# Softcap attention followed by a leaky two-matmul layer, on one core: the instruction order planned anew, with another landing model for transfers and a later load of the slopes

## The chip, the cores and the metric

One core of one Trainium2 chip runs the whole program. The metric is device time in microseconds, and less is better. The engines named below are PE (TensorE, matmuls and transposes), DVE (VectorE), ACT (ScalarE), POOL (GpSimd) and SP (SyncE, which issues the loads).

## The reference

Attention over 4 batches of 12 heads, 448 tokens and 64 wide, whose output, laid out as 1792 tokens of 768, goes through a matmul, a leaky activation with one slope for each of 2048 hidden columns, and a second matmul:

```
scores = scale * np.matmul(q, k.transpose(0, 1, 3, 2))
scores = cap * np.tanh(scores / cap)
scores = scores - np.max(scores, axis=-1, keepdims=True)
attn = np.exp(scores)
attn = attn / (np.sum(attn, axis=-1, keepdims=True) + 1e-09)
x = np.matmul(attn, v)  ->  (1792, 768)
h = x @ w_in                                            # (1792, 2048)
g = np.maximum(h, 0.0) + alpha * np.minimum(h, 0.0)     # alpha: the slopes
out = (g @ w_out).astype(np.float32)                    # (1792, 768)
```

q, k and v come in 32-bit floats, w_in and w_out in 64-bit ones, so a block of 128 rows or columns of a weight is a load of 768 KB.

## The kernel before

**Numbers.** A value that goes into a large matmul is split into a high and a low half of 16 bits (hi = the rounded value, lo = value minus hi), and products are added up in three passes. A split is written in one of two forms. The two-step form is a scaled cast (`scaled`, on ACT L430, POOL L432 or DVE L434) and then one DVE instruction that scales again and subtracts (`split_lo`, L440). The three-step form scales in 32 bits (the same three lines), casts (`copy`, ACT L424 or DVE and POOL L426) and subtracts (`minus`, DVE or POOL, L437). The constants `QA` and `PA` say which share of the splits of q and k (batches 2 and 3) and of the blocks of P, the normalised attention (`turn_split`), takes the two-step form. A 64-bit weight is first turned into 32 bits by three DVE instructions on its words (L1059, L1063, L1069, in tiles `wi` and `wp`).

**Stages.** First q, k and v of batch 0 are loaded, with w_in between them. The attention of batch 0 runs in 32 bits: q and k turned (L542, PE), scores (L577, PE), tanh (L614, ACT), row maxima (L618, DVE), exp (L625, ACT), P turned (L729, PE, and copied out of PSUM into `ptall` by L424 or L426), P times V (L792 or L775, PE). Beside it w_in is turned to 32 bits, normed (L1094, PE, or L1083, ACT; maxima by L393, DVE) and split (L440). Then the first matmul of batch 0 (called mm1, L958, on tiles `wi` and `xring`) runs in pieces beside the attention of batch 1, whose q and k come through `rqk` and L896. Its leaky activation ends in DVE L968 (tile `gr`). While it runs, w_out is loaded, turned to 32 bits, normed and split. The second matmul (mm2, L999, on `wp` and `gall`) of batch 0 follows, and so on to mm2 of batch 3.

**Maxima over all partitions** (`allmax`) are a chain of four steps: a PE transpose (L410), a DVE reduction (L406, for several columns also L408), a PE matmul that spreads the result (L413), and one DVE step that takes it. `g_scales` runs such a chain for the slopes: DMA L1160 into `alph`, maximum L393 (into `small`), the chain, and five small DVE steps to L1175, which make the two columns that the leaky activation reads.

**What sets the order.** All work is given to a planner (class `Plan`) as operations with a priority and a duration for each engine that may run it. To each priority comes an entry of the table `OFF`, picked by the operation's tag. At build time the planner runs the list forward: whenever an engine is free it takes the ready operation of lowest priority, and where two engines may run it, one of them by penalties (`PEN`, `PEN2`, `PENP`). On PE it may prefer an operation of the kind that ran last, if its priority is within `SAME` of the best. For a load it keeps a time `dma` to which the queue is filled, and takes the load to have landed a fixed 1000 ns after its turn. When PE finds nothing ready, a PSUM bank is free and the planned time is under `FILL_END`, it issues a dummy matmul (`fill`, L1234). The order that comes out is fixed: on the chip each engine executes its own list in that order and waits by semaphores where a list runs ahead of another. No line of the program changes at run time.

Of the kernel before, what the change touches and what calls it, by code (L numbers as in the profile page):

```python
# [28 lines left out]
PEN = 24324.02  # L29
PEN2 = 429.82  # L30
PENP = 13233.71
B0_P = 250.67
LD_P = -207.13
LO_P = 1890.42
MM_P = 6687.03
X_P = 667.61
ST_P = 117.78
ST1_P = -42.95
PV_P = 180.1
QK_P = -338.71  # L40
V_P = 252.08
WI_P = -374.93
WI_S = -48.3
A_S = 13.82
MM1_P = 493.59
WO_P = -142.86
WO_S = 62.91
WT_P = -1745.7
WT_S = 152.86
B1_P = 620.29  # L50
B_S = 132.46
EVAC_P = -1002.09
# [14 lines left out]
QA = 1.0  # L67
# [5 lines left out]
SAME = 531.89  # L73
LOAD_C = (600, 1400, 800)
# [5 lines left out]
PA = 0.25  # L80
# [4 lines left out]
OFF = [3.2, -401.1, 51.6, -139.2, 1454.6, 45.4, 49.8, -38.2, -674.3, -24.9, 39.6, 25.1, 158.3, -197.5, -914.5, -88.5, 509.5, -178.6, 60.3, 0.0, -1155.4, -66.4, -213.9, -817.7, 80.9, 223.2, -262.7, 162.2, -263.5, -63.5, -48.8, 49.8, -256.2, 272.2, -674.8, -1321.6, 1531.5, 161.9, 273.3, 23.0, 228.0, 224.1, 138.3, 162.3, -70.6, 30.6, -8.0, -59.3, 30.1, -251.0, -100.4, 5.5, -69.7, 0.0, 190.4, 1595.1, -152.2, 194.8, -431.9, -189.3, -1491.2, -862.4, 160.4, -1336.1, 33.2, -298.2, 425.3, -180.6, 0.0, 254.3, -23.0, -3.7, 263.9, -37.4, -38.9, -2097.2, -19.9, -1.4, -1522.5, -29.8, 647.0, -1770.0, 0.0, 0.0, -2980.8, 103.4, 1914.1, -557.4, 537.1, 33.2, 0.0, -723.6, -373.5, 666.0, 575.6, -2208.6, 45.7, 308.9, -17.0, 277.2, -3.3, -236.9, -75.7, -356.6, -424.1, -182.7, -3431.1, 182.9, 247.3, 272.4, 199.8, 432.4, 188.3, 97.9, 326.3, -20.1, 35.8, 424.1, -507.3, -84.4, -664.4, -36.3, -30.7, 155.2, -3774.1, -4705.4, -2233.8, -2244.6, -3489.6, -1814.7, -1501.8, -3152.5, -2525.4, -6577.6, -3901.4, -7294.4, -6281.6, -5181.6, -5400.1, -5863.8, -9408.1, -4749.4, 31.4, -11.9, 122.6, -3734.2, -450.2, 1153.7, -124.3, -50.9, -94.9, 6155.4, 2068.9, -169.5, -343.4, -8404.7, -9228.1, -8931.4, -5436.4, -4226.4, -3789.6, -4921.0, -5305.1, -3359.5, -409.5, -2852.4, 56.1, -4291.1, -4249.4, -2856.7, -4858.0, -4928.0, -3627.5, -1585.6, -3201.7, -1945.6, -301.3, -781.1, 155.4, -5983.9, -3358.0, -3814.4, -282.7, 13.0, 89.7, 103.9, -3.1, 445.1, -30.9, -43.1, -148.3, -92.7, -159.7, -48.8, 183.8, -1697.3, -20.0, -2624.2, -1773.8, -5.0, -2469.5, 7.9, -2409.3, -2334.6, -16.3, -17.6, -2663.0, -2434.4, -2901.0, -2971.5, -2452.3, -655.0]  # L85
# [9 lines left out]
class Plan:  # L95
# [44 lines left out]
    def order(self):  # L140
        now, dma, seq = START, 0.0, 0
# [54 lines left out]
        while todo:  # L196
# [10 lines left out]
            for e in free:  # L207
# [3 lines left out]
                while ready[e]:  # L211
# [23 lines left out]
                    if e == "sp":  # L235
                        issue, wait, t = t
                        dma = max(now + wait, dma) + t
                        end = dma + 1000.0
                        lanes = lanes[1:] + [end]
                        free[e] = max(now + issue, lanes[0])  # L240
                    elif e == "pe":
                        free[e] = run_pe(t + (SWITCH + o.first if o.mode != mode else 0.0), o.rows)
                        mode = o.mode
                        end = free[e] + DRAIN
# [35 lines left out]
def kernel(  # L280
# [11 lines left out]
    nc = tc.nc  # L292
# [163 lines left out]
    def load(prio, dst, src, b, pair, w):  # L456
        op(prio, {"sp": (600, 1400, 880)}, lambda e: nc.sync.dma_start(out=dst.rearrange("p (h c) -> p h c", h=2),
                                                          in_=heads(src, b, pair)), w=w)
# [581 lines left out]
    def load_w(prio, flat, fr, i, src, split):  # L1040
# [6 lines left out]
        op(prio, {"sp": (550, 1800, (2350 if split else 1950) if wide else 1700)}, lambda e: nc.sync.dma_start(  # L1047
# [110 lines left out]
    def g_scales(prio):  # L1158
        plan.tag = -1
# [48 lines left out]

    def all_ops():
        loads32()  # L1210
        g_scales(30)
        for part in range(2):
            attention_0(part)
        for j in range(0, NF, WG):
# [67 lines left out]
```

## Time and profile before

| what | value |
|---|---|
| time, median of 3 runs | 673.92 us (673.86 to 675.18) |
| the profiled execution | 677.45 us, of which 675.7 us from the first to the last instruction (its span) |
| PE busy | 648.9 us, 96% of the span; mean granted clock 0.996 |
| DVE busy | 460.8 us (68%) |
| ACT busy | 418.3 us (62%) |
| POOL busy | 269.3 us (40%) |
| loads and stores | 87.06 MB |

An engine's busy time is the union of its instructions' spans, so waiting is not in it. The granted clock is the share of full speed that TensorE was given: 1.00 is 2.4 GHz and 0.50 is 1.2 GHz. The profiled execution lies 3.5 us above the median of the timed runs.

### The profile page before, as it was taken

How to read it: one execution, taken by the hardware profiler on the slowest of the kernel's cores; microseconds unless marked ns; L12 is line 12 of the kernel's file. 1: busy time of each engine (PE TensorE's matmuls, PEld its weight loads, DVE VectorE, ACT ScalarE, POOL GpSimd, SP SyncE). 2: the span in 40 equal slices, each digit the busy share in tenths (PEclk: the TensorE clock that was granted, in tenths of full speed). 3: DMA queues.
4: the chain of work that ended last, by engine and by line, in shares of the span. 5: the costliest groups of instructions: out<-in, count | busy, mean ns of one | idle time of the engine just before them, and what ended most of it. 6: DMA issues, size and time to landing. Idle time of an engine off the chain costs nothing. (4 is left out here: it accounts for less than half of the span.)

```text
span 675.7 us, 13258 instructions
## 1 busy us (share of the span) xinstructions
PE 648.9 (96%) x5003; PEld 410.0 (61%) x5003; DVE 460.8 (68%) x886; ACT 418.3 (62%) x868; POOL 269.3 (40%) x395
## 2 busy tenths in 40 slices
PE   8979988999999998999999999999999999999997
PEld 6768767788776555544455555544445555555664
DVE  2898999899898886688988787788884004440000
ACT  3868899789989955487867478686884013331000
POOL 0233267558777723174763445466671000000000
PEclk9999999999999999999999999999999999999999
DMA  9997945434863699558589889789766100000110
GB/s 231 277 275 180 305 131 146 149 109 151 185 92 64 115 185 194 137 104 145 94 160 205 162 190 176 146 157 161 121 104 117 40 24 25 1 0 1 30 41 23
DMA packets 190048, 87.06 MB, mean 129 GB/s; under 512 B 156256, under 2 KB 186272, under 8 KB 189984
## 3 DMA queue, kind: packets, MB, share of 16 engines
q1 hardware_dynamic: 189760, 86.12, 58.9%
q8 instruction: 39, 0.64, 0.4%
q14 instruction: 25, 0.20, 0.1%
q10 hardware_dynamic: 224, 0.10, 0.1%
HBM read 45.82 MB, written 5.51 MB: 76 GB/s over the span
## 5 line engine op out<-in xcount | busy, mean ns | idle before, releaser
L958 PE MATMUL p<-xring,wi 128*128 128x448 f16 (+2 forms) x1440 | 226.9, 315 | 2.8 <-DVE gr L968 1.7
L999 PE MATMUL p<-wp,gall 128*128 128x384 f16 x1344 | 223.9, 326 | 0.6 <-DVE gr L968 0.6
L958 PEld LDWEIGHTS <-wi 128*128 128x128 f16 x1440 | 134.7, 98 | 87.6 <-issue 9.1
L999 PEld LDWEIGHTS <-gall 128*128 128x128 f16 x1344 | 129.9, 98 | 90.2 <-issue 6.0
L625 ACT ACTIVATE tall<-tall,mxs 128x448 f32<-128x448 f32 x126 | 82.9, 660 | 24.1 <-POOL mxs L620 15.0
L968 DVE SCALAR_TENSOR_TENSOR gr<-p,ca_g,gr 128x448 f32<-128x448 f32 (+2 forms) x80 | 46.8, 585 | 58.4 <-ACT gr L430 58.0
L618 DVE TENSOR_REDUCE mxs<-tall 128x2 f32<-128x896 f32 x63 | 67.9, 1080 | 8.9 <-ACT tall L614 8.5
L620 POOL TENSOR_SCALAR mxs<-mxs,small 128x2 f32<-128x2 f32 x68 | 38.7, 570 | 60.3 <-DVE mxs L618 52.7
L437 POOL TENSOR_TENSOR pw<-tall,pw 128x448 f16<-128x448 f32 x47 | 52.5, 1123 | 21.8 <-ACT pw L424 20.5
L430 ACT ACTIVATE gr<-p,cs_g 128x448 f32<-128x448 f32 (+2 forms) x63 | 35.1, 556 | 39.5 <-PE p L958 37.3
L430 ACT ACTIVATE wp<-p,small 128x384 f32<-128x384 f32 x21 | 12.1, 577 | 65.6 <-PE p L999 65.3
L437 POOL TENSOR_TENSOR gall<-gr,gall 128x192 f16<-128x192 f32 (+4 forms) x52 | 43.9, 848 | 15.8 <-ACT gall L424 11.3
L644 POOL TENSOR_SCALAR rr<-sums 128x2 f32<-128x2 f32 (+2 forms) x70 | 25.1, 360 | 57.0 <-ACT tall L625 35.0
L614 ACT ACTIVATE tall<-s,ams 128x896 f32<-128x896 f32 x42 | 41.5, 995 | 9.0 <-POOL pw L437 4.2
L775 PE MATMUL p<-ptall,vs 112*64 112x448 f16 x384 | 41.1, 354 | 3.2 <-DMA ptall<-pw 1.8
L434 DVE TENSOR_SCALAR wp<-p,joint 128x384 f32<-128x384 f32 (+1 forms) x2 | 1.0, 512 | 60.4 <-ACT wp L430 60.4
L424 ACT ACTIVATE pw<-tall 128x448 f16<-128x448 f32 x51 | 28.7, 571 | 20.9 <-DMA ptall<-pw 18.6
L424 ACT ACTIVATE gall<-gr 128x384 f16<-128x384 f32 (+4 forms) x62 | 27.4, 448 | 21.1 <-DVE gr L968 20.7
L437 DVE TENSOR_TENSOR pw<-tall,pw 128x448 f16<-128x448 f32 x37 | 24.5, 665 | 14.9 <-ACT pw L424 13.6
L775 PEld LDWEIGHTS <-vs 112*64 112x64 f16 x384 | 21.9, 109 | 20.5 <-issue 7.9
L437 DVE TENSOR_TENSOR gall<-gr,gall 128x64 f16<-128x64 f32 (+4 forms) x60 | 27.5, 464 | 6.9 <-ACT gall L424 4.4
L432 POOL TENSOR_SCALAR tall<-tall,rr 128x448 f32<-128x448 f32 x32 | 25.3, 792 | 13.5 <-DVE rr L647 12.5
(173 smaller groups left out, 983.5 us busy)
## 6 DMA issues: line engine op xcount, KB each, us to landing
wp<-in_moe_w_in_dram SPq DMA_DIRECT2D x16, 768.0 KB, 9.1
wp<-in_moe_w_out_dram SPq DMA_DIRECT2D x16, 768.0 KB, 4.5
rvs<-in_v_dram SPq DMA_DIRECT2D x38, 224.0 KB, 3.7
rqk<-in_k_dram SPq DMA_DIRECT2D x12, 224.0 KB, 3.4
rqk<-in_q_dram SPq DMA_DIRECT2D x12, 224.0 KB, 3.2
ptall<-pw SPq DMA_TRANSPOSE x128, 3.2
wp<-in_q_dram SPq DMA_DIRECT2D x6, 224.0 KB, 8.6
wp<-in_k_dram SPq DMA_DIRECT2D x6, 224.0 KB, 8.7
```

The lines of the kernel that those rows point to most:

```text
L424: nc.scalar.activation(out=o, in_=i, func=AF.Copy)
L430: nc.scalar.activation(out=o, in_=i, func=AF.Copy, scale=s)
L432: nc.gpsimd.tensor_scalar(out=o, in0=i, scalar1=s, scalar2=1.0, op0=ALU.mult, op1=ALU.mult)
L437: (nc.gpsimd if e == "pool" else nc.vector).tensor_tensor(out=o, in0=a, in1=b, op=ALU.subtract)
L614: op(pr, {"act": (152 if reg else 245) + 377 * 2}, lambda e: nc.scalar.activation(out=t, in_=s[:, :, :S].rearrange("p c (j k) -> p c j k", ...
L618: op(pr, {"dve": 136 + 469 * 2}, lambda e: nc.vector.tensor_reduce(out=mt, in_=t, axis=AX.XY, op=ALU.max), r=tr, w=[mr], port=False)
L620: op(pr, {"dve": 200, "pool": 265}, lambda e: (nc.gpsimd if e == "pool" else nc.vector).tensor_scalar(out=mt, in0=mt, scalar1=ncap, scalar ...
L625: nc.scalar.activation(out=t[:, x], in_=t[:, x], func=AF.Exp, scale=capr, bias=mt[:, x:x + 1], accum_out=sums[:, u.idx % 3, col + x:col + ...
L775: nc.tensor.matmul(pv[x * D:(x + 1) * D, :n], vs[:, z, c:c + D], u.pt[x][:CP, y * NCH + kc], start=(i == 0), stop=(i == len(prods) - 1))
L958: nc.tensor.matmul(ps_p[h.slot][:, :n], w[:, z, kk, :], x[:, d, o:o + n], start=(kk == 0 and z == d), stop=(kk == NPAIR - 1 and z == 1))
L968: op(pr, {"dve": 198 + 1.07 * n}, lambda e: nc.vector.scalar_tensor_tensor(out=t, in0=ps_p[h.slot][:, :n], scalar=ca_g[:, j:j + 1], in1=t, ...
L999: nc.tensor.matmul(ps_p[h.slot][:, :NH], g[j][:, d, t * P:(t + 1) * P], w[:, z, hf * NH:(hf + 1) * NH], start=(j == 0 and z == d), stop=(j ...
```

## The change

Nothing is computed otherwise, apart from the form of some splits. What changes are numbers that set the order, and two rules:

- The planner's landing model. `deep` is how far the queue of loads is filled ahead of this load; a load now lands 1200 ns, plus half of `deep` up to 1600 ns, after its turn. A load of 224 KB counts 940 ns in the queue (880 before), one of w_in 2550 (2350), of w_out 2050 (1950), of the slopes 3200 (900), and the 112 KB loads of q and k in batches 1 to 3 (`LOAD_C`) 850 (800).
- `g_scales` has priority 2300 instead of 30 and a tag of its own.
- `QA` goes from 1.0 to 0: all 24 splits of q and k in batches 2 and 3 take the three-step form. `PA` goes from 0.25 to 0.75: of the 112 blocks of P, 84 take the two-step form, 28 before.
- `SAME` goes from 531.89 to 1872.02, and 22 base priorities and penalties and the whole table `OFF` (now 213 entries) have other values.

```diff
-PEN = 24324.02
-PEN2 = 429.82
-PENP = 13233.71
+PEN = 17613.56
+PEN2 = 1129.33
+PENP = 11360.55
...
-QA = 1.0
+QA = 0
...
-SAME = 531.89
-LOAD_C = (600, 1400, 800)
+SAME = 1872.02
+LOAD_C = (600, 1400, 850)
...
-PA = 0.25
+PA = 0.75
...
+                        deep = max(0.0, dma - now - wait)
                         dma = max(now + wait, dma) + t
-                        end = dma + 1000.0
+                        end = dma + 1200.0 + min(1600.0, 0.5 * deep)
...
     def load(prio, dst, src, b, pair, w):
-        op(prio, {"sp": (600, 1400, 880)}, lambda e: nc.sync.dma_start(out=dst.rearrange("p (h c) -> p h c", h=2),
+        op(prio, {"sp": (600, 1400, 940)}, lambda e: nc.sync.dma_start(out=dst.rearrange("p (h c) -> p h c", h=2),
...
-        op(prio, {"sp": (550, 1800, (2350 if split else 1950) if wide else 1700)}, lambda e: nc.sync.dma_start(
+        op(prio, {"sp": (550, 1800, (2550 if split else 2050) if wide else 1700)}, lambda e: nc.sync.dma_start(
...
     def g_scales(prio):
-        plan.tag = -1
-        op(prio, {"sp": (500, 1100, 900)}, lambda e: nc.sync.dma_start(out=alph, in_=alpha.rearrange("(j p) -> p j", p=P)), w=[("sg", 0, 1)])
+        plan.tag = 211
+        op(prio, {"sp": (500, 1100, 3200)}, lambda e: nc.sync.dma_start(out=alph, in_=alpha.rearrange("(j p) -> p j", p=P)), w=[("sg", 0, 1)])
...
-        g_scales(30)
+        g_scales(2300)
```

One line is added, so from L237 on every line of the changed kernel has a number one higher.

**On SP, the end of batch 0's loads.** Before, from the 16th row of SP's list on (`wp_93` to `wp_96` take turns at holding w_in; `wp_97` to `wp_100` hold q and k of batch 0, and later w_out):

```order
L457 DMA wp_98<-in_k_dram 112x2x256
L457 DMA vs_119<-in_v_dram 112x2x256
L1047 DMA wp_96<-in_moe_w_in_dram 128x6x256
L1047 DMA wp_93<-in_moe_w_in_dram 128x6x256
L457 DMA wp_100<-in_q_dram 112x2x256
L1047 DMA wp_95<-in_moe_w_in_dram 128x6x256
L1160 DMA alph<-in_moe_alpha_dram 128x16x1
L457 DMA wp_100<-in_q_dram 112x2x256
L1047 DMA wp_97<-in_moe_w_out_dram 128x1536
```

Afterwards, the same stretch of SP's list:

```order
L458 DMA wp_100<-in_q_dram 112x2x256 x2
L1048 DMA wp_93<-in_moe_w_in_dram 128x6x256
L458 DMA rvs<-in_v_dram 112x2x256
L458 DMA vs_119<-in_v_dram 112x2x256
L458 DMA xring<-in_v_dram 112x2x256
L1048 DMA wp_95<-in_moe_w_in_dram 128x6x256
L1161 DMA alph<-in_moe_alpha_dram 128x16x1
L1048 DMA wp_97<-in_moe_w_out_dram 128x1536
```

The last load of q has moved from behind the slopes to four loads ahead of them. At the head of the list, five loads of q and k now stand ahead of the first of w_in, three before.

**On PE, the chain of the slopes.** Before, with the scores of the last heads of batch 0 behind it (`p_63` to `p_66` are the PSUM banks, `n_wi` are the maxima of w_in):

```order
L413 MATMUL p_65<-mxt,ones 128x4
L542 MATMUL p_63<-ident,wp_100 64x112 x8
L410 MATMUL p_65<-ident,small 1x128
L413 LDWEIGHTS ones
L413 MATMUL p_65<-mxt,ones 128x1
L577 MATMUL s_61<-tall,wp_100 128x224 x4
```

Afterwards:

```order
L411 MATMUL p_63<-ident,vam 1x128
L414 LDWEIGHTS ones
L414 MATMUL p_63<-mxt,ones 128x1
L411 MATMUL p_63<-ident,small 1x128
L414 LDWEIGHTS ones
L414 MATMUL p_63<-mxt,ones 128x1
L730 MATMUL p_64<-ident,gall 112x128 x4
L730 MATMUL p_66<-ident,gall 112x128 x4
L411 MATMUL p_63<-ident,n_wi 4x128
```

The chains of v's maximum (`vam`), of the slopes and of the next norms of w_in now stand behind each other with eight transposes between them, and no dummy matmul among them. In the whole list the dummy matmuls go from 175 to 106.

**On DVE, beside the early pieces of mm1.** Before, the steps up to the leaky activation that frees the PSUM bank of the next piece of mm1, which is on wi_81 and stands behind 83.6 us of PE's own work:

```order
L387 TENSOR_SCALAR iv_wi<-p_66 128x4
L440 SCALAR_TENSOR_TENSOR wi_84<-wi_86,s_wi,wi_84 128x768
L618 TENSOR_REDUCE mxs<-ptall 128x2
L389 TENSOR_SCALAR iv_wi<-iv_wi 128x4
L440 SCALAR_TENSOR_TENSOR wi_87<-wi_89,s_wi,wi_87 128x768
L968 SCALAR_TENSOR_TENSOR gr<-p_66,ca_g,gr 128x192
```

Afterwards, the steps up to a copy of turned P in batch 1, which PE needs behind 84.3 us of its own work:

```order
L409 TENSOR_SCALAR mxt<-ident,mxt 4x4
L441 SCALAR_TENSOR_TENSOR wi_88<-wi_90,s_wi,wi_88 128x768
L388 TENSOR_SCALAR iv_wi<-p_65 128x4
L812 TENSOR_TENSOR xs<-p_66,xs 128x256
L390 TENSOR_SCALAR iv_wi<-iv_wi 128x4
L1060 TENSOR_SCALAR wp_93<-wp_94 128x768
L1140 RECIPROCAL s_wi<-iv_wi 128x4
L1064 SCALAR_TENSOR_TENSOR wp_93<-wp_94,wp_93 128x768
L619 TENSOR_REDUCE mxs<-tall 128x2
L394 TENSOR_REDUCE vam<-p_64 128x1
L648 RECIPROCAL rr<-rr 128x4
L427 COPY ptall<-p_66 112x4x128
```

The attention of batch 1 has moved ahead of pieces of mm1 (an engine's own work is the sum of its instructions in the list at the mean durations of their groups in the profile before, dummy matmuls left out): 72 matmuls of L958 stand within the first 83.6 us of PE's own work before, and within the first 100.1 us afterwards.

## Rows read from the trace of the kernel before

**Rows 1.** Page, part 1: busy us (share of the span) xinstructions.
```profile
PE 648.9 (96%) x5003; PEld 410.0 (61%) x5003; DVE 460.8 (68%) x886; ACT 418.3 (62%) x868; POOL 269.3 (40%) x395
```
**Rows 2.** The chain that ended last: start us, us, what.
```profile
504.42 7.96 PE p L999 x48
...
608.90 62.41 PE p L999 x384
```
**Rows 3.** Windows: stretch, its us, busy of each engine (count), PEclk, DMA share, GB/s.
```profile
0.00:80.00 80.00, 70.26 (x865) 59.64 (x865) 61.74 (x115) 56.35 (x120) 19.93 (x43) 0.98 0.95 248
80.00:160.00 80.00, 73.37 (x758) 61.27 (x757) 74.39 (x131) 68.63 (x159) 49.89 (x61) 1.00 0.50 151
160.00:300.00 140.00, 136.02 (x1040) 88.79 (x1038) 117.18 (x225) 107.19 (x221) 80.35 (x111) 1.00 0.68 134
300.00:520.00 220.00, 217.99 (x1456) 114.36 (x1455) 179.26 (x351) 159.05 (x324) 119.13 (x183) 1.00 0.81 149
...
660.00:675.70 15.70, 11.30 (x70) 6.58 (x68) 0.42 (x1) 1.00 (x2) 0.00 (x0) 0.94 0.11 25
```
**Rows 4.** Windows of L1234 alone, the dummy matmuls, in the first 80 us.
```profile
0.00:80.00 80.00, 13.54 (x173) 11.94 (x173) 0.98 0.95 248
```
**Rows 5.** Windows of 20 us, two of the first eight; columns as in group 3.
```profile
60.00:80.00 20.00, 19.12 (x235) 17.05 (x232) 19.91 (x34) 16.72 (x39) 6.13 (x8) 1.00 0.88 243
...
140.00:160.00 20.00, 19.16 (x210) 17.10 (x208) 19.93 (x34) 16.19 (x43) 12.79 (x16) 1.00 0.40 120
```
**Rows 6.** Waits of PE, 0 to 400 us: waited for: us, times, longest.
```profile
PE p L542 <- DMA wp<-in_q_dram: 3.0, 3, 1.3
...
PE p L958 <- DVE gr L968: 1.7, 2, 0.8
...
PE p L775 <- issue: 1.3, 1, 1.3
...
PE p L410 <- DVE vam L529: 1.0, 2, 0.8
...
PE p L775 <- DMA ptall<-pw: 0.7, 1, 0.7
```
**Rows 7.** Timeline of PE about 152 us: start, us, instruction [idle before it].
```profile
152.55 0.82 PE L958 MATMUL p<-xring,wi 128*128 128x192 f16 x8 [0.84 <-DVE gr L968]
```
**Rows 8.** Timeline of DVE, 114 to 118 us.
```profile
114.94 0.68 DVE L426 COPY ptall<-p 112x512 f32<-112x512 f32 x1
```
**Rows 9.** Waits of DVE, 0 to 207 us; columns as in group 6.
```profile
DVE wi L1059 <- DMA wp<-in_moe_w_in_dram: 8.8, 5, 4.6
...
DVE wp L1059 <- DMA wp<-in_moe_w_out_dram: 2.5, 2, 1.6
```
**Rows 10.** Timeline of DVE, 9 to 18 us.
```profile
9.58 0.56 DVE L1059 TENSOR_SCALAR wi<-wp 128x768 int32<-128x768 int32 x1 [4.57 <-DMA wp<-in_moe_w_in_dram]
```
**Rows 11.** Groups of DVE by form: line, shapes, count | busy us, mean ns.
```profile
L440 DVE SCALAR_TENSOR_TENSOR nat<-rqk,ams,nat 112x256 f16<-112x256 f32 x48 | 27.1, 614 | 0.1
L437 DVE TENSOR_TENSOR pw<-tall,pw 128x448 f16<-128x448 f32 x37 | 24.5, 665 | 14.9 <-ACT pw L424 13.6 <-POOL pw L426 0.9
L440 DVE SCALAR_TENSOR_TENSOR pw<-tall,rr,pw 128x448 f16<-128x448 f32 x28 | 19.9, 711 | 3.3 <-ACT pw L430 3.3
```
**Rows 12.** Timeline of PE, 36 to 46 us.
```profile
38.72 0.99 PE L542 MATMUL p<-ident,wp 112*64 112x112 f32 x16 [0.75 <-DMA wp<-in_q_dram]
...
40.49 1.78 PE L577 MATMUL s<-tall,wp 64*128 64x224 f32 x16
```
**Rows 13.** Windows about a pause of PE; columns as in group 3.
```profile
46.00:48.40 2.40, 0.00 (x0) 0.01 (x1) 2.40 (x3) 2.13 (x6) 1.80 (x3) 1.00 1.08 323
48.40:50.00 1.60, 1.58 (x12) 1.40 (x14) 1.60 (x4) 0.15 (x1) 0.97 (x1) 0.75 1.09 343
50.00:52.00 2.00, 2.00 (x13) 1.38 (x9) 1.34 (x2) 0.92 (x1) 0.00 (x0) 0.50 1.15 279
```
**Rows 14.** Timeline of PE, 45 to 53 us.
```profile
48.93 3.14 PE L577 MATMUL s<-tall,wp 64*128 64x224 f32 x16
```

More of the change, by code (lines that the diff above doesn't have):

```diff
@@ L28 @@
 AQ = 3
-PEN = 24324.02
-PEN2 = 429.82
-PENP = 13233.71
[L32 to L52, printed above, removed]
+PEN = 17613.56
+PEN2 = 1129.33
+PENP = 11360.55
+B0_P = 663.82
+LD_P = -321.77
+LO_P = 2106.39
+MM_P = 6096.43
+X_P = 624.32
+ST_P = 167.74
+ST1_P = -107.3
+PV_P = -101.81
+QK_P = -455.54
+V_P = 329.3
+WI_P = -299.53
+WI_S = -31.69
+A_S = 17.19
+MM1_P = 379.27
+WO_P = 157.32
+WO_S = 41.37
+WT_P = -2099.18
+WT_S = 16.53
+B1_P = 412.84
+B_S = 112.23
+EVAC_P = -1314.66
 LAT = 35.0
@@ new lines @@
+OFF = [342.6, -7.7, -9.1, 0.0, 807.2, 220.9, 0.1, -403.5, 323.1, 393.5, 0.0, 767.6, 677.3, 0.0, -463.9, 290.4, 349.0, -81.1, -18.5, -174.2, -729.8, -2084.7, -344.3, -55.5, -233.5, 178.9, 107.2, 0.0, -269.8, 0.0, -46.0, 470.5, 37.4, -33.6, -485.0, -14.4, 5306.2, 807.0, 7.2, 3536.3, 1985.2, 272.7, 4709.4, 168.0, 228.4, 1474.8, 3.7, 0.0, -5.9, -810.1, 0.0, -1.6, -559.8, -239.5, 2763.1, 176.5, 176.2, 133.4, 158.2, 136.8, 120.1, -9.3, 257.6, 650.2, 1063.2, -172.3, 52.1, -157.2, 31.7, -53.8, 29.9, 230.0, -1253.5, -685.2, -1.2, -3319.8, -1110.3, -3965.3, -5249.8, -47.2, -722.4, -459.9, -69.5, -11.9, -231.9, -1298.0, -888.9, -936.5, 2.0, 29.5, 821.0, 0.0, -487.3, 903.8, -241.8, 167.6, 154.8, 27.3, -154.0, -366.0, -424.8, -2192.9, -2021.7, -2141.0, -2584.3, -3193.3, -2956.4, -1776.7, -1206.1, -3754.8, -1921.8, -211.4, -2488.5, -2829.9, -1665.6, -2469.6, -595.1, -1496.7, -314.8, -1544.2, -3233.1, -2498.4, -1610.3, -1731.7, -1159.6, -1943.8, -1530.0, -1547.0, -1332.0, -1201.3, -130.1, -886.1, -590.1, 623.2, -72.5, -361.2, -129.3, -136.5, -932.1, -253.9, -1492.2, -50.7, -85.7, -34.0, 1158.5, 503.2, -1042.2, 651.6, 72.9, 10.7, 0.0, 2733.6, -403.7, 4746.4, -300.0, -12344.4, -12239.7, -14208.6, -10298.3, -5122.2, -4318.0, -5166.3, -6295.0, -4082.2, -258.8, -3271.3, -149.7, -5007.8, -264.1, -0.8, 298.2, -5522.1, -3915.9, 605.5, 642.8, -4.7, 361.7, 924.6, 426.0, -5199.4, -3321.6, -3754.8, -202.3, 444.7, -50.9, 0.0, 3.4, 191.8, 98.2, 73.2, -76.0, 214.6, 0.0, -182.7, -245.5, 372.0, 333.2, 2693.0, 281.9, 1329.2, 224.4, 164.1, 181.1, 2334.3, 908.9, 232.1, 756.7, -838.1, 525.8, 252.5, 544.3, 180.5, -236.4]
```

1 line of the change is left out of this document (removed).

## The prediction

> **What bounds the kernel now.** I read the busy times, then the chain of waits, then windows. PE is busy for 648.9 of 675.7 us [rows 1], and from 504.42 us on the chain is little but PE [rows 2]. So any gain or loss is in the time in which PE does not do its own work. The windows say where that lies [rows 3]: PE is idle for 9.7 us up to 80 us, 6.6 from 80 to 160, 4.0 from 160 to 300, 2.0 from 300 to 520 and 4.4 in the tail. To these come the dummy matmuls, 13.5 us, nearly all in the first 80 us [rows 4]: they fill time in which PE has nothing else, so I count them as stall. Up to 160 us PE's stall is thus 9.7 + 6.6 + 13.5 = 29.9 us, and behind that, without the tail, 6.0.
>
> Who makes PE stall? In the 20 us from 60 and again from 140 DVE is busy for 19.9 [rows 5], while PE idles, and the last such pause is PE's wait of 0.84 us at 152.55 for a DVE step [rows 7]. Up to there DVE is the bound. Most of the waits named for PE before that are short, and some of them are put down to loads [rows 6]. A load that comes late costs only what DVE does not cost anyway.
>
> This gives a sum that can be carried to another order. At a place where PE waits for DVE, PE's stall so far is DVE's work up to the step waited for, plus the time that DVE has lost, minus PE's own work ahead of the waiting matmul. The works are counts in the order by the mean durations of their groups. At 152.55 us, DVE's work ahead is 134.2 us and PE's 123.3, so DVE has lost 152.55 - 134.2 = 18.4, the lag (work against work) is 10.8, and the stall 29.2; the windows had 29.9, so such sums hold to within 0.7. Elsewhere in this stretch the lag of before is 7 to 10 us.
>
> **The change part by part.** *The sizes first.* PE's own work is the same in both orders. DVE's grows from 460.8 to 465.2 us, ACT's falls by 14.0 and POOL's by 31.0. This comes from `QA` and `PA`. Of the q and k splits, 48 DVE steps of 614 ns go, 29.5 us; of the P blocks, 56 more DVE steps of 711 ns come, 39.8, and 24 subtractions of 665 ns go, 16.0 [rows 11]; smaller shifts between engines give the rest. All of these steps stand behind 159 us of DVE's own work in either order, so they run from about 167 us on. From 160 to 520 us PE idles for 6.0 us altogether and DVE is free for 360 - 296.4 = 63.6 [rows 3]. I take the forms as worth nothing; if that cover were gone, they would cost at most their 4.4 us, and if POOL's 31 us less shorten the waits left there, they give at most the 1.5 us that remain under the covers counted below.
>
> *The slopes' load.* It moves to behind q, k and v, as all its list on SP shows. The last load of q, which stood behind it, was waited for 0.75 us [rows 12]. So the move is worth 0 to 0.75 us, and only if nothing else holds PE there. DVE bounds this stretch, so I take 0. (The Trainium skill, page "DMA: Bandwidth & Descriptors", section "Queues, rings and completion order", says that completion is not first in, first out for one issuing engine, so a small load could overtake. By that rule the slopes held nobody up and the move gives exactly 0; no row here shows an overtaking.)
>
> *The slopes' chain.* It stands on PE's list right behind that of v's maximum, with the norms next. PE's own work there is 1.7 us (38.9 to 40.6 of its total) while DVE has 7 us between the answers; there is no dummy matmul in it. This is counted in the lag, which climbs from -0.2 to 6.2 us across it. It isn't the largest lag and so costs nothing by itself.
>
> *The order on DVE and PE.* This is the term that decides. The attention of batch 1, which needs much of DVE for little of PE, has gone ahead of mm1, which needs little of DVE. At 84 us of PE's own work, DVE's work that must be done was 91.6 us (lag 8.0) and is now 99.9 (lag 15.6). At 103 and 115.6 us of PE's work the lag is 15.1 and 15.2; only behind 160 does it fall to 10.6, then 7.7 at 196. The largest lag of before was 10.8.
>
> What DVE loses is to be taken over, as no row shows it for the new order. At 99.3 us of its work it was at 115.62 us [rows 8], lost 16.3; at 134.2 us it had lost 18.4. The main loss is at the start: the first weight is waited for until 9.58 us [rows 10]. Now two loads more stand ahead of that weight. At the 248 GB/s of the first 80 us [rows 3], 2 x 224 KB (229,376 bytes each) take 1.8 us. Some 0.8 of it should be won back, since DVE next waits for the first exps in either order; so I add 0 to 1.8 and take 0.4 at the later places. The two places give 15.6 + 16.3 + 0.4 = 32.3 and 15.2 + 18.4 + 0.4 = 34.0. The larger one holds: 34.0 against 29.2, **+4.8 us** when the second matmul starts (bounds +4.4 to +6.2).
>
> *What comes back.* Of the 6.0 us of stall behind 160 us, the waits for DVE's small steps and for one transposed P, 2.7 us in all (0.83 of it the longer `vam` wait, 0.7 the `ptall` one [rows 6]), fall away when PE comes 4.8 us later against the same DVE. The wait of 1.3 that shows no releaser, and 2.0 in many small pieces, I leave as they are. So -2.7 (bounds 0 and -6.0). The tail of 4.4 us is the same mm2 and evictions.
>
> Sum: +4.8 - 2.7 = **+2.1 us**. The profiled execution would have a span of 677.8 instead of 675.7; it lies 3.5 us above the median of 673.92, so I set the sum on the median: 676.0 us. With the bounds of the two terms it lies between 4.4 - 6.0 = -1.6 and +6.2, mostly 674 to 678.7.
>
> **The rivals.** *DVE's waits go (faster).* The landing model is nearer to what the queue does. DVE's waits for w_in are 8.8 us, 4.6 of them the first, and it waits 2.5 for w_out [rows 9]. If the new order asks for each weight late enough, the 4.2 us of the later w_in waits vanish: DVE loses 14.2 instead of 18.4 at the second place and the stall there is 15.2 + 14.2 = 29.4, with 15.6 + 14.2 = 29.8 at the first one. Against 29.2 that is +0.6, and -2.7 behind it: 671.8; with all of the 6.0 gone, 668.5. For it speaks that loads of w_in get a little more room in SP's list; against it that two fifths of those waits are under 0.8 us each. The turning point is a loss of 16.7 us at 131 us of DVE's work: below it the change is faster.
>
> *All is won back (same).* If the lag of 15 us is paid but the whole 6.0 behind it goes, it is -1.2: 672.7; with half of the unreleased waits, 674.
>
> *The clock (slower).* After a pause of 2.4 us without a dummy matmul, PE was granted 0.75 and then 0.50 (1.2 GHz) [rows 13], and 16 score matmuls took 3.14 us [rows 14] against 1.78 [rows 12]. 69 dummy matmuls fewer leave such pauses open. (The Trainium skill, page "TensorE: Matmul & The Clock Gate", section "Part 1: The HAM clock gate", has the throttled clock as the default state, which activity releases; that speaks against taking fillers out, and the rows just named agree.) Where PE waits for DVE anyway a slow stretch costs nothing; where scores go through ACT to DVE it delays DVE. Two such stretches at 1.4 us each on top of the forecast: 678.8.
>
> *The change does not do what it says.* The slopes' load could be no hindrance: then only the order counts, which is my forecast without change.
>
> **How the numbers follow.** What a measurement of this kernel can tell from no change is about 0.2%, 1.35 us: same is 672.57 to 675.27. Forecast 0.47 (676.0, of which a fourth falls into same), waits go 0.25 (671.8, nearly all faster), all won back 0.15 (674, same), clock 0.13 (678.8, slower). Faster: 0.25 and 0.01 from the won-back case, 0.26. Same: 0.12 + 0.13 = 0.25. Slower: 0.35 + 0.13 + 0.01 = 0.49. The range leaves a tenth on either side: below 670.8 lies the part of the faster rival in which most of the 6.0 goes too, above 680.0 the clock rival with the upper bound of the lag.
>
> **What would show it.** Right: PE idle or on dummy matmuls for about 34 us up to the first L999, which has 177.3 us of PE's own work ahead of it and so would start near 211 us (by the same sum 177.3 + 29.2 = 206.5 before); its waits in the region of 110 to 150 us end with DVE steps; DVE over 19 busy in most windows of 20 us from 60 to 140; next to no PE idle behind 160. Wrong, to the fast side: DVE's waits for w_in summing to under 6 us, and a first L999 at or before 207.5 us. Wrong, to the slow side: granted clocks under 0.9 in more than one window of 20 us. It would also be wrong if the mean durations did not hold in the new order, for instance if DVE's steps beside POOL's took longer or shorter.

## The result, and the profile after

The changed kernel takes 666.33 us (median of 4 runs, 665.50 to 667.37) against 673.89 of the kernel before; the ratio is 0.9889, with a 95% interval of 0.9865 to 0.9913. It is faster by 7.6 us, where 2.1 us slower was forecast, and lies below the range that was given.

The profiled execution has a span of 665.6 us (675.7 before). Page, part 1, of the changed kernel (answers to [rows 1]):

```profile
PE 642.9 (97%) x4934; PEld 406.2 (61%) x4934; DVE 469.8 (71%) x885; ACT 407.0 (61%) x839; POOL 245.8 (37%) x369
```

The same windows as [rows 3], the last one moved with the end of the span (stretch, its us, busy of PE, PEld, DVE, ACT and POOL, then PEclk, DMA share, GB/s):

```profile
0.00:80.00 80.00, 69.06 (x816) 57.33 (x817) 65.94 (x124) 58.05 (x123) 26.49 (x46) 0.96 0.94 254
80.00:160.00 80.00, 75.70 (x794) 63.43 (x793) 77.94 (x138) 76.34 (x179) 47.77 (x65) 1.00 0.51 154
160.00:300.00 140.00, 139.18 (x1050) 89.56 (x1048) 123.60 (x228) 100.81 (x204) 77.98 (x112) 1.00 0.71 139
300.00:520.00 220.00, 217.74 (x1453) 116.00 (x1452) 174.75 (x332) 145.89 (x291) 93.60 (x148) 1.00 0.78 148
...
650.00:665.60 15.60, 11.22 (x70) 6.56 (x67) 0.42 (x1) 1.00 (x2) 0.00 (x0) 0.96 0.11 26
```

And the dummy matmuls alone, L1235 here (answers to [rows 4]):

```profile
0.00:80.00 80.00, 8.88 (x105) 7.79 (x105) 0.96 0.94 254
```

PE's stall up to 160 us is 10.9 + 4.3 + 8.9 = 24.1 us, where it was 29.9. From 160 to 520 us it is 0.8 + 2.3 = 3.1 instead of 6.0. The tail is the same 4.4. So of the 10.1 us between the two profiled executions 5.8 lie ahead of 160 us, 2.9 behind it, and 1.3 are PE's own work (642.9 less 9.1 of dummy matmuls, 633.8, against 648.9 less 13.8, 635.1).

Who is busy in the first part is seen best in windows of 20 us. First three of the kernel before that the prediction did not show, then the same stretches of the changed kernel:

```profile
40.00:60.00 20.00, 17.16 (x172) 14.23 (x172) 16.53 (x32) 15.67 (x32) 8.05 (x14) 0.91 0.95 266
80.00:100.00 20.00, 17.65 (x172) 13.81 (x172) 17.33 (x32) 17.78 (x40) 11.15 (x17) 1.00 0.55 166
120.00:140.00 20.00, 18.27 (x189) 15.57 (x187) 17.88 (x33) 16.22 (x39) 10.62 (x11) 1.00 0.52 173
```

```profile
40.00:60.00 20.00, 12.91 (x117) 9.82 (x117) 19.10 (x43) 14.37 (x33) 8.66 (x10) 0.84 1.04 308
...
80.00:100.00 20.00, 18.66 (x186) 14.54 (x184) 19.96 (x34) 19.38 (x43) 9.80 (x14) 1.00 0.65 199
...
120.00:140.00 20.00, 18.85 (x204) 16.93 (x202) 19.13 (x36) 17.53 (x43) 9.73 (x14) 1.00 0.49 154
```

DVE is the third column. Before, it sat idle for 2.1 to 3.5 us in each of these stretches; afterwards for 0.0 to 0.9. Its steps last as long as before (the 17 row maxima of `gall`: a mean of 1073 and 1071 ns), so DVE is further on by waiting less. Waits of DVE up to 207 us in the changed kernel, against [rows 9]:

```profile
DVE wi L1060 <- DMA wp<-in_moe_w_in_dram: 6.6, 2, 6.2
```

Behind the first weight it waits 0.4 us for w_in, where it was 4.2, and not at all for w_out, where it was 2.5.

### The profile page after: what moved, and what is told of

The parts are those of the page before. It is cut to its first block, busy times and chain, and to the rows that moved or that the text cites. A ratio compares the mean times of both kernels' runs of the same rounds, so it can differ in the third digit from the quotient of the medians.

```text
span 665.6 us, 13056 instructions
## 1 busy us (share of the span) xinstructions
PE 642.9 (97%) x4934; PEld 406.2 (61%) x4934; DVE 469.8 (71%) x885; ACT 407.0 (61%) x839; POOL 245.8 (37%) x369
## 4 chain that ended last, share of the span: by engine, by line
PE 55%; DMA 2%; DVE 2%; ACT 1%; issue 1%; SPq 0%; DVEq 0%; ACTq 0%
PE p L959 25%; PE p L1000 23%; PE p L776 4%; PE s L584 3%; DMA ptall<-pw 2%; DMA rqk<-in_k_dram 1%; DVE small L394 1%; DVE mxs L619 0%; DVE pw L441 0%; PE p L411 0%; ACT tall L626 0%; PE p L414 0%; DVE pw L435 0%; ACT tall L615 0%; DVE nat L438 0%
## 5 line engine op out<-in xcount | busy, mean ns | idle before, releaser
L959 PE MATMUL p<-xring,wi 128*128 128x448 f16 (+2 forms) x1440 | 224.3, 315 | 0.8 <-DVE iv_wi L388 0.8
L621 POOL TENSOR_SCALAR mxs<-mxs,small 128x2 f32<-128x2 f32 x70 | 43.6, 623 | 80.0 <-DVE mxs L619 66.8
L441 DVE SCALAR_TENSOR_TENSOR pw<-tall,rr,pw 128x448 f16<-128x448 f32 x84 | 60.0, 725 | 8.6 <-ACT pw L431 7.9
L438 POOL TENSOR_TENSOR gall<-gr,gall 128x256 f16<-128x256 f32 (+4 forms) x50 | 37.2, 746 | 19.4 <-ACT gall L425 12.2
L645 POOL TENSOR_SCALAR rr<-sums 128x2 f32<-128x2 f32 (+2 forms) x70 | 23.1, 330 | 57.0 <-ACT tall L626 41.5
L431 ACT ACTIVATE pw<-tall,rr 128x448 f16<-128x448 f32 x46 | 30.3, 664 | 16.4 <-DMA ptall<-pw 9.9
L776 PE MATMUL p<-ptall,vs 112*64 112x448 f16 x384 | 39.4, 354 | 0.0
L438 DVE TENSOR_TENSOR gall<-gr,gall 128x384 f16<-128x384 f32 (+3 forms) x62 | 30.1, 486 | 4.7 <-ACT gall L425 1.8
L584 PE MATMUL s<-qkTs 64*128 64x448 f16 (+1 forms) x288 | 28.1, 352 | 0.6 <-ACT tall L615 0.6
L427 POOL CAST gall<-gr 128x192 f16<-128x192 f32 (+4 forms) x28 | 19.0, 681 | 24.4 <-DVE gr L969 22.5
```

Of the source, the lines that this page charges most:

```text
L431: nc.scalar.activation(out=o, in_=i, func=AF.Copy, scale=s)
L438: (nc.gpsimd if e == "pool" else nc.vector).tensor_tensor(out=o, in0=a, in1=b, op=ALU.subtract)
L441: nc.vector.scalar_tensor_tensor(out=o, in0=i, scalar=s, in1=hi, op0=ALU.mult, op1=ALU.subtract)
L584: yield lambda z=z, w=w: nc.tensor.matmul(s[rows, x, :S], q[a, z * S + cols.start:z * S + cols.stop], q[a, w * S:(w + 1) * S], start=(z == ...
L621: op(pr, {"dve": 200, "pool": 265}, lambda e: (nc.gpsimd if e == "pool" else nc.vector).tensor_scalar(out=mt, in0=mt, scalar1=ncap, scalar ...
L776: nc.tensor.matmul(pv[x * D:(x + 1) * D, :n], vs[:, z, c:c + D], u.pt[x][:CP, y * NCH + kc], start=(i == 0), stop=(i == len(prods) - 1))
```

## Experiments

The measure used below is DVE's loss: the time at which it ends the step with 98.7 us of its own work ahead of and in it, less 98.7. In the changed kernel that step ends at 107.0 us, so the loss is 8.4 (by unrounded works); before it ended at 115.0, 16.3. The works are those of the prediction. The steps are, before and afterwards:

```profile
114.01 1.01 DVE L440 SCALAR_TENSOR_TENSOR wi<-wi,s_wi,wi 128x768 f16<-128x768 f32 x1
```

```profile
105.96 1.08 DVE L619 TENSOR_REDUCE mxs<-tall 128x2 f32<-128x896 f32 x1
```

By the windows DVE is idle for 21.7 us up to the first and for 14.1 up to the second. The level differs from that of the loss, which rests on mean durations; the difference, 7.5 us, is close to the 7.9 of the losses.

Ratios are to the kernel before on the same chip. The changed kernel itself was timed on another occasion than the experiments; repeated once among them it took 669.33 us against 675.65 for the kernel before, 0.9906. So ratios between 0.989 and 0.993 are not told apart below.

| run | DVE's loss, us | ratio (95% interval) |
|---|---|---|
| kernel before, the profile shown / another | 16.3 / 12.2 | 1 |
| before_alpha_late | 13.6 | 1.0011 (0.9982 to 1.0041) |
| before_no_fill | 12.8 | 0.9969 (0.9937 to 1.0001) |
| before_short_win | 9.8 | 0.9956 (0.9935 to 0.9978) |
| before_start | 9.7 | 0.9989 (0.9956 to 1.0022) |
| before_start_short | 8.8 | 0.9951 (0.9920 to 0.9982) |
| before_loads_after | 17.6 | 1.0070 (1.0042 to 1.0099) |
| changed kernel, the profile shown / another | 8.4 / 10.4 | 0.9889 (0.9865 to 0.9913) |
| after_short_win | 8.5 | 0.9918 (0.9889 to 0.9947) |
| after_no_fill | 8.9 | 0.9903 (0.9872 to 0.9934) |
| after_alpha_early | 11.0 | 0.9909 (0.9875 to 0.9943) |
| after_w0_fourth | 12.5 | 0.9926 (0.9897 to 0.9955) |
| after_loads_before | 18.0 | 1.0017 (0.9996 to 1.0039) |

### Does DVE bind? Extra work on it

```diff
+            n += e == "dve"
+            if e == "dve" and 40 <= n < 160 and n % 15 == 10:
+                self.extra()
...
+    def extra():
+        for i in range(4):
+            nc.vector.tensor_reduce(out=spare[:, i:i + 1], in_=ident, axis=AX.X, op=ALU.max)
```

> The kernel before with 32 extra maxima over 128 columns on DVE (written to a tile nobody reads, so the result is untouched), four at each of eight places between its 40th and 145th planned DVE step; some 0.25 us each, 8 us of DVE work. Theory A (DVE bounds PE up to 152 us in the kernel before, but with idle time of its own, 9.2 us between 40 and 152.5 us, in which it waits for loads and for ACT): part of the 8 us is swallowed by that idle time, +3 to +6 us. Theory B (my prediction's reading, DVE is bound there and its losses are fixed): +8 us. Theory C (something else sets PE's stall): under +2 us.

> The changed kernel with the same 32 extra maxima on DVE at the same counts of DVE steps, 8 us of DVE work. DVE was idle for only 2.4 us between 40 and 142.8 us there. Theory A and theory B: +6.5 to +8 us, more than in the kernel before by A, the same by B. Theory C: under +2 us.

Measured: 1.0030 (1.0006 to 1.0055), +2.0 us (0.4 to 3.7), in the kernel before, and 0.9969 (0.9946 to 0.9992) in the changed one, which is 0.8% or 5.4 us above the changed kernel itself (some 3 to 8 by the two intervals). The extra steps were 6.8 us of DVE (group of DVE by form, in dve8_before):

```profile
L1245 DVE TENSOR_REDUCE spare<-ident 128x1 f32<-128x128 f32 x32 | 6.8, 269 | 0.0
```

In the kernel before DVE's idle time from 40 to 152.5 us went from 9.2 to 3.4 us:

```profile
40.00:152.50 112.50, 102.60 (x1081) 85.96 (x1082) 109.11 (x215) 94.86 (x214) 56.03 (x75) 0.98 0.64 185
```

So in the changed kernel some four fifths of the extra DVE work reach the end, and in the kernel before under a third. Where these steps stand, DVE binds the changed kernel; the kernel before is held by it only here and there, and its idle time swallows the rest. The prediction's reading (B, +8 us in the kernel before) falls. Theory A has the direction, but both of its ranges, set for 8 us of extra work, were too high, and for the kernel before the interval does not exclude theory C (under +2 us). One caution: of the 5.5 us between the profiled spans of the changed kernel without and with the extra work, 2.5 are idle time of PE and 3.0 are busy time, and from 40 to 60 us the granted clock was 0.76 with the extra work and 0.84 without. So a part of the cost reached the end as slower work of PE.

### The order of the loads alone

```diff
+        want = [...]
+        at = sorted(key[x] for x in want)
+        new = [todo[key[x]] for x in want]
+        for i, x in zip(at, new):
+            todo[i] = x
```

In `want`, shortened here, stand the first 25 loads in the order that is asked for: in the first two runs that of the other kernel.

> The kernel before, every list as it is, but the first 25 loads of SP in the changed kernel's order (five q and k ahead of the first w_in, all of batch 0's q and k ahead of the slopes). Theory L (the order of the loads made the gain, since DVE's waits for loads and for the first exps shrink): 667 to 670 us. Theory O (the order of the work on DVE and PE made it, which puts ready work where DVE waited): 672.5 to 675.5 us.

> The changed kernel, every list as it is, but the first 25 loads of SP in the order of before, the slopes ahead of the last q again. Theory L: 671 us or more, with DVE's waits for w_in and the first exps back. Theory O: 665.5 to 669 us.

Measured: 1.0070 and 1.0017. Neither order of loads gains anything under the other kernel's lists, so neither theory holds as put: L is right that the loads decide in the changed kernel (all of its gain goes without them), and wrong that they would help the old lists. Where the lists wait is in the waits up to 160 us. With the old lists and the new loads:

```profile
PE p L515 <- DMA rvs<-in_v_dram: 3.9, 1, 3.9
```

With the new lists and the old loads:

```profile
PE p L561 <- DMA wp<-in_q_dram: 5.6, 4, 2.9
```

The old lists want v early and the new ones q. In these two kernels an order of loads has a value only together with the lists that wait for it.

> The changed kernel, every list as it is, but the first load of w_in two places earlier in SP's list, as in the kernel before (behind three loads of q and k instead of five). DVE waits 6.2 us for it and is then busy nearly all the time. Theory D (DVE's work and lost time set PE's stall, whatever else): the first step on w_in is 1.6 us earlier and the time falls by 1 to 1.6 us, to 664.7 to 665.5 us. Theory M (the lists are matched to the order of the loads, so two q loads that come later cost what the weight wins): 666 to 669 us.

Measured: 0.9926 (0.9897 to 0.9955). Theory D, by which the earlier weight makes the changed kernel faster (664.7 to 665.5 us, 0.986 to 0.988 of the time before), is refuted. Whether it makes it slower can't be told: the intervals overlap, and the profiled execution, with a span of 670.2 us, is one of the slowest of seven. In it the first weight was waited for 5.0 us instead of 6.2, but DVE's next step then waited for the scores:

```profile
DVE wi L1078 <- DMA wp<-in_moe_w_in_dram: 5.0, 1, 5.0
DVE mxs L637 <- ACT gall L633: 4.6, 1, 4.6
```

By 40 us DVE had done 23.4 us of work, where it was 27.2 in the changed kernel, and at the later step its loss was 4.1 us greater: what it lost at the start was still lost there. This is the mechanism of theory M.

### The slopes' load

> The kernel before, every list as it is, but the slopes' load one place later in SP's list, behind the last load of q. Theory N (8 KB hold nobody up): 673 to 675 us. Theory S (they hold up the q behind them): up to 0.75 us less by the wait for that q, more by whatever else follows, 672.5 us or less.

> The changed kernel, every list as it is, but the slopes' load moved up in SP's list by eight loads, ahead of the last two loads of q. Theory S (the slopes' load, which took 10.3 us to land in the kernel before, holds up what is queued behind it): the last q, the v loads and w_in land later, 667.5 us or more, by over 0.2%. Theory N (8 KB hold nobody up): 665 to 667.5 us, the same as the changed kernel.

Measured: 1.0011 and 0.9909. Moved back one place in the kernel before, the load makes no difference that can be seen (0.9982 to 1.0041). Moved up in the changed kernel (by seven places, not eight; five loads stand there between the last q and the slopes, not four) it is 0.2% above it, with intervals that overlap, and a span of 666.1 against 665.6. That is just the bound between the two theories, so this run does not decide; in the kernel before theory N is the better one. The move of the slopes is no visible part of the gain.

### Late weights

```diff
-    load_w(prio + LD_P, flat, fr, j % 4, src_wi(j), True)
+    load_w(prio + LD_P, flat, fr, j % 4, src_wi(j), True, DM // P if j < 4 else 1)
```

The new last argument is how many of a block's six chunks are loaded.

> The kernel before, every list as it is, but the loads of w_in from the fifth on bring one sixth of each block (128 KB instead of 768; the rest of the tile keeps older numbers, so 12 blocks of w_in are not the real ones); all other work is done in full. The queue of loads is then 7.5 MB shorter and what lands from about 35 us on lands earlier. Theory A (up to 150 us DVE and PE of the kernel before lose time on loads that land late: DVE some 5 us on weights behind the first, PE 2.4 us on q of batch 1): 667 to 670 us. Theory B (DVE's losses there are fixed by the chain of the attention and not by loads): 672.5 us or more.

> The changed kernel with the same short loads of w_in (12 blocks are not the real ones). DVE waited for loads of weights for 0.4 us behind the first one, PE for none. Theory A: 665 to 667.5 us, no change. Theory B: no change either. A gain of more than 2 us would say that loads still hold the changed kernel up in a place that its waits do not name.

Measured: 0.9956, 3.0 us less (1.5 to 4.4), in the kernel before; 0.9918 in the changed kernel, whose interval takes in its own 0.9889: no gain. DVE in the kernel before, from 40 to 80 us, with the short loads:

```profile
40.00:80.00 40.00, 38.25 (x435) 32.52 (x437) 39.79 (x72) 35.61 (x77) 17.39 (x25) 1.00 0.47 122
```

It is busy for 39.8 of 40 us there; with the full loads it was for 36.4. Its loss falls to 9.8. So late loads cost the kernel before some 3 us of time, and nothing that shows in the changed kernel. The gain in the kernel before is clear of noise, which speaks for theory A; but its 671.55 us lie between the ranges of A and B, so the effect is smaller than A had it.

### The start

> The kernel before, every list as it is, but the first six loads of SP in the changed kernel's order: five of q and k, then the first w_in. Theory Q (the first scores and exps come some 2.5 us earlier, and DVE, which waited 3.3 us for them, loses that much less): 671 to 673 us, with the first tanh at about 11 us instead of 13.7. Theory W (DVE loses 1.6 us more on the first weight, and the later waits for weights swallow the rest): 673.5 to 676 us.

> Both at once: the first six loads of the kernel before in the changed kernel's order, and the short loads of w_in from the fifth on (12 blocks are not the real ones). Theory Q with theory A (late q and k at the start and late weights are the whole of what DVE lost): DVE's loss at 98.7 us of its work falls to 7 to 8.5 us, and the time to 668 to 670 us, since the stall behind 160 us stays as before. Rival (the lists themselves are the rest): no better than the short loads alone, 671 to 672.5 us.

Measured: 0.9989 and 0.9951. The first is unclear. Its ten runs lie between 669.9 and 678.5, and the profiled one was the fastest of them, in which the loads also ran faster (first 80 us):

```profile
0.00:80.00 80.00, 71.92 (x905) 61.53 (x907) 64.75 (x119) 59.78 (x128) 24.12 (x46) 1.00 0.98 268
```

268 GB/s against 248 in [rows 3]. So its small loss can't be put down to the edit. The first tanh came at 14.8 us, later than before (13.7), so theory Q's mechanism is refuted for the old lists, and PE's timeline tells why:

```profile
13.25 0.52 PE L1112 MATMUL p<-wi 128*128 128x128 bf16 x6 [1.19 <-DVE wi L1087]
13.70 1.78 PE L595 MATMUL s<-tall,wp 64*128 64x224 f32 x16
```

The old list has the norms of the first weight (L1112 here) ahead of the first scores (L595), so the scores wait until DVE has turned that weight to 32 bits, and a later weight makes them later. In the changed kernel's list the scores come first (PE's timeline there; L1095 are the norms):

```profile
9.88 1.78 PE L578 MATMUL s<-tall,wp 64*128 64x224 f32 x16
...
15.48 0.52 PE L1095 MATMUL p<-wi 128*128 128x128 bf16 x6
```

There the first tanh comes at 11.0 us. Both edits together give no more than the short loads alone, though DVE's loss is then 8.8, nearly that of the changed kernel. In that run PE's stall up to 160 us was 22.4 us (8.9 idle, 13.5 dummies), less than in the changed kernel, and it was still idle for 6.8 us from 160 to 650. Neither edit of the loads mends these us behind 160; the changed lists have 3.1 there. The rival, by which the lists themselves are the rest, is right (671.04 us). As far as one execution each shows, the new lists are better than the old ones with mended loads only behind 160 us, and not ahead of it.

### Dummy matmuls

```diff
-                    started.append((now, lambda _, slot=banks[-1]: self.fill(slot), e))
+                    started.append((now, lambda _, slot=banks[-1]: self.fill(slot), "fill"))
...
-            fn(e)
+            if e != "fill":
+                fn(e)
```

> The kernel before, every list as it is, without its 175 dummy matmuls (13.8 us of PE). Theory H (they stand in time that PE has to wait anyway): 673 to 676 us, with more idle time instead. Theory I (they delay PE's own work, so 69 fewer of them are a part of the gain): 671 us or less. Theory J (they hold the clock up, and PE's slower stretches go on to DVE): 676 us or more, with granted clocks under 0.9 in two or more of the first four stretches of 20 us.

> The changed kernel, every list as it is, without its 106 dummy matmuls (some 9 us of PE). Theory H: 665 to 668 us. Theory I: 664 us or less. Theory J: 668 us or more, with lower granted clocks up to 60 us.

Measured: 0.9969 and 0.9903. Theory H holds for the changed kernel; for the kernel before, the interval runs from no change to 0.6% less, and the 672.81 us lie between H and I. Theory J, a loss by a lower clock, is refuted in both. In the changed kernel PE's granted clock falls while it waits in the chains of maxima (windows of 3 us):

```profile
50.00:53.00 3.00, 0.39 (x4) 0.13 (x2) 3.00 (x5) 1.63 (x6) 0.50 (x1) 1.00 1.18 258
53.00:56.00 3.00, 0.53 (x2) 0.18 (x2) 2.81 (x11) 2.18 (x5) 0.00 (x0) 0.58 0.80 226
56.00:59.00 3.00, 2.88 (x13) 1.96 (x15) 2.91 (x9) 1.92 (x5) 2.36 (x3) 0.50 1.08 362
```

PE is busy for 0.9 us in six and then has a granted clock of 0.50, 1.2 GHz, for 3 us, while DVE is busy for 8.7 of the 9. That PE would have waited for DVE there at any clock is inferred from DVE's busy time.

### The landing model and the forms, planned anew

In the first run (`after_model_old`) the planner has its old landing model and its old costs of loads again:

```diff
-                        deep = max(0.0, dma - now - wait)
                         dma = max(now + wait, dma) + t
-                        end = dma + 1200.0 + min(1600.0, 0.5 * deep)
+                        end = dma + 1000.0
```

In the other two it has the old shares of the forms, and in the last of them the dummy matmuls planned behind 120 us are left out as well:

```diff
-QA = 0
+QA = 1.0
...
-PA = 0.75
+PA = 0.25
```

> The changed kernel with the planner's old landing model and old costs of loads (a load lands 1000 ns after its turn); table, priorities and forms stay changed, and the planner makes another order from them. Theory P (the gain comes from an order that plans for loads that land late): DVE's waits for w_in come back, 669 to 675 us. Theory T (it comes from the table and the priorities, the model matters little): 665.5 to 668.5 us.

> The changed kernel with the old shares of split forms (QA 1.0, PA 0.25); everything else stays changed, and the planner makes another order from them. DVE's work falls by some 9 us and ACT's and POOL's grow, all behind 160 us, where PE is idle for 3.1 us in the changed kernel and was for 6.0 before. Theory F (the forms are hidden): 665.5 to 668.5 us. Theory G (POOL's slower steps come back into the waits behind 160 us): 669 us or more.

> The changed kernel planned with the old shares of split forms, but without the 168 dummy matmuls that the planner then puts behind 160 us (10.7 us of PE). Theory K (those dummies, which delay PE's own work there, were the loss, the forms are hidden): 665.5 to 669 us. Theory G (POOL's slower steps hold PE up, with idle time in place of the dummies): 674 us or more.

Measured: 1.0263 (1.0220 to 1.0306), 1.0073 (1.0047 to 1.0100), and 1.0117 (1.0073 to 1.0160). Either part, taken out of the changed kernel, leaves it slower than the kernel before. The first run's 692.68 us lie above the ranges of both P and T. One wait up to 160 us does most of it:

```profile
PE p L1094 <- DVE vam L387: 15.0, 1, 15.0
```

That is not a load that came late: DVE's waits for w_in were 8.0 us, 2.1 of them beside the longest one (0.4 in the changed kernel, 4.2 in the kernel before), and from 40 to 80 us it was busy for 38.8. PE stood for 15 us in the chain of v's maximum, since this plan has put a row of conversions and splits of weights ahead of the step that ends that chain on DVE's list. So what P names came back in part, but it is not what cost the time. With the old forms, the stretch from 160 to 230 us is the one that suffers; first without the extra dummies, then in the changed kernel:

```profile
160.00:230.00 70.00, 60.73 (x514) 46.34 (x512) 62.69 (x116) 55.17 (x117) 49.10 (x64) 0.90 0.64 128
```

```profile
160.00:230.00 70.00, 69.59 (x591) 52.38 (x589) 66.88 (x115) 53.92 (x107) 45.75 (x60) 1.00 0.58 116
```

PE is idle for 9.3 us, waiting for tanh of batch 2 and for the maxima of its q and k, though no engine is busier than DVE's 62.7. Neither run lies in the range of theory F, that the forms are hidden. Theory K, that the dummies were the loss, is refuted: without them it is no faster. (The granted clock of this stretch was 1.00 with them and 0.90 without.) The times are those of theory G, but whether the old forms or the order that the planner made from them cost the time stays open. These three runs show that a part of the change can't be priced by planning without it: the planner then makes another order throughout.

### The same kernels again

> The kernel before, unchanged, profiled once more. Theory R (its waits for loads move with the rate at which the loads come): DVE's loss at 98.7 us of its work is more than 1.5 us away from 16.3 unless the first 80 us again move 248 GB/s and its time is again near 677; faster loads go with a smaller loss and a shorter time. Rival (the loss belongs to the order): 15.5 to 17 us, whatever the rate.

> The changed kernel, unchanged, profiled once more. Theory R: DVE's loss at 98.7 us of its work is 8 to 10 us again, whatever the rate of the loads, and the time 665 to 668 us. Rival: it moves by as much as that of the kernel before.

Measured: 673.79 us and a loss of 12.2 at 256 GB/s for the kernel before, 669.33 us and 10.4 at 248 GB/s for the changed one. DVE's loss is no fixed number of an order: it moved by 4.1 us in the kernel before and by 2.0 in the changed kernel. So theory R is right for the kernel before; for the changed kernel both its bounds (10 us of loss, 668 us) were passed. The profile from which the prediction took 16.3 was one at the slow end; that of the changed kernel is the slowest of its four.

## Why the prediction was wrong, point by point

**The bound.** That what counts is the time in which PE doesn't do its own work is right, and the windows show the gain there. That DVE is the bound up to 152 us in the kernel before was read from two windows of 20 us in which DVE is busy for 19.9 [rows 5]. They were the fullest of eight; the three shown above, 16.5 to 17.9, say the opposite, and the extra DVE work confirms it: under a third of it reached the end. The two largest of PE's waits up to 160 us were for loads of q. One is in [rows 6]; the other is not:

```profile
PE p L896 <- DMA rqk<-in_q_dram: 2.4, 1, 2.4
```

**The lag** was counted as the lists have it. Timelines of DVE and of PE at the copy of turned P that the prediction named, in the changed kernel:

```profile
107.24 0.66 DVE L427 COPY ptall<-p 112x512 f32<-112x512 f32 x1
```

```profile
108.53 1.73 PE L793 MATMUL p<-ptall,nat 112*64 112x256 f32 x14
```

The copy ends at 107.9 us, 23.6 us more than the 84.3 of PE's own work. That this equals 15.6 + 8.0 is no test: the loss is defined by the time at which the step ends, so it must. PE did not even stand still there: it shows no idle time from its transposes at 107.3 us to L793. The test is the stall in the windows, 24.1 us up to 160 us; the sum for the second place, 15.2 + 8.4 = 23.6, comes within 0.5 of it. So lag and loss do add up to the stall, once the loss is known.

**What DVE loses, "to be taken over", is the step that failed.** 16.3 + 0.4 and 18.4 + 0.4 were put in; 8.0 and about 8.4 were measured (18.4 and 8.4 with 134 us of DVE's work done). The term was +4.8 us where the stall fell by 5.8, 10.6 us between them; the forecast missed by 9.7. The first matmul of mm2, before and afterwards:

```profile
206.54 4.06 PE L999 MATMUL p<-wp,gall 128*128 128x384 f16 x24
```

```profile
200.36 5.80 PE L1000 MATMUL p<-wp,gall 128*128 128x384 f16 x33
```

It starts at 200.4 us, with 200.4 - 177.3 = 23.1 us of stall ahead of it and not 34.0. Two things were wrong in it. First, lag and loss are not apart: an order that puts more of DVE's work ahead of PE's has a larger lag just because DVE has ready work where it waited before. DVE was idle for 9.2 us from 40 to 152.5 us before and for 2.4 from 40 to 142.8 afterwards:

```profile
40.00:80.00 40.00, 36.29 (x404) 31.29 (x403) 36.44 (x65) 32.39 (x70) 14.19 (x22) 0.96 0.92 255
80.00:152.50 72.50, 65.92 (x678) 54.32 (x677) 66.89 (x119) 62.30 (x145) 43.03 (x54) 1.00 0.50 149
```

```profile
40.00:80.00 40.00, 31.97 (x325) 26.20 (x324) 38.74 (x76) 30.57 (x67) 18.80 (x24) 0.91 0.90 268
80.00:142.80 62.80, 58.76 (x606) 48.94 (x605) 61.66 (x108) 59.64 (x137) 36.19 (x47) 1.00 0.53 159
```

Second, part of the loss was the loads of that one execution. Short loads took 3.0 us off the kernel before, and its loss differed by 4.1 us between two profiles.

**The first weight.** +0.4 us was set for two loads more ahead of it. It did come later (waited for until 11.3 us instead of 9.6), but PE's new list has the first scores ahead of that weight's norms, so the first tanh ran at 11.0 instead of 13.7 us, and this wait of DVE, behind the first weight of the kernel before, went:

```profile
DVE tall L426 <- ACT gall L614: 3.3, 1, 3.3
```

The weight put back gained nothing (0.9926), so the cost that was set for its delay is not borne out.

**What comes back** behind 160 us: -2.7 forecast, -2.9 measured. That the number came true is luck. The reason given was that PE comes 4.8 us later against the same DVE; its first matmul of mm2 came 6.2 us earlier. What went are not only the waits that were named, but all 1.8 us of waits for transposed P and the 1.3 without a releaser, which was to stay; and one wait grew, from 0.7 us:

```profile
PE p L411 <- DVE small L394: 1.7, 2, 1.0
```

Why they went is open.

**The slopes**: 0 to 0.75 us forecast at 0; no difference was measured. Their load did not overtake: in both traces it landed 0.7 us behind the load issued ahead of it. **The forms**: worth nothing by the forecast; the runs can't say. Their sum was off: the steps that are listed come to -5.7 us of DVE's work, so the "smaller shifts" that lead to its +4.4 are 10.1 us, and DVE's busy time grew by 9.0 (460.8 to 469.8).

**The rivals.** The faster one, "DVE's waits go", is what happened, at a chance of 0.25, and its own 671.8 was too high by 5.5: it let only the 4.2 us of later w_in waits vanish, where DVE's loss fell by 10.0. Its turning point (a loss of 16.7 at 131 us of DVE's work) was passed by 8 us. The clock rival did not occur: one stretch of 20 us had a granted clock under 0.9, 40 to 60 us with 0.84 (0.91 before), and there DVE was busy for 19.1.

**The signs.** The first L999 at 200.4 us, under 207.5, was the sign that told. The other one for the fast side did not come: the waits for w_in were 6.6 us, not under 6. And a sign of being right did come, DVE over 19 busy in the windows from 60 to 140 us, so it could not tell the forecast from its rival.

## What to carry to other kernels

When an order is planned anew, the work ahead of each wait can be counted from the lists, but the idle time of the engine that is waited for can't be taken over: it is made by the old order. Look at that engine in every window, not at its fullest ones, and ask which of its pauses the new order has ready work for. Loads and lists can be tuned to each other: here the new order of loads under the old lists was slower than either kernel, and the old one under the new lists took all of the gain.

## What the runs showed of the hardware that was not expected

The rate at which loads move differs from run to run: 248 and 256 GB/s in the first 80 us of two executions of the kernel before, 268 in one with the same bytes and six loads in another order. Their spans were 675.7, 672.0 and 668.1 us; that the rate is the cause is not shown. 25 runs of the kernel before on one chip lay between 670.6 and 679.9 us. The changed kernel's four lay within 1.9 us, but its later repeat took 2.0 us more than the slowest of them. In all of the five executions that were looked at for it, the loads of SP's queue landed in the order of issue, the 8 KB of the slopes too, 9.9 to 10.3 us after it. The removal of 9.1 and of 13.8 us of dummy matmuls left no trace in the time that is clear of noise. TensorE's granted clock fell to 0.50 for 3 us while DVE was busy for 8.7 of 9 us; what that fall cost was not measured by itself.
